# Weights of experts 2 and 3, gathered rows and one store at other places of the load queue

## The chip, the cores and the metric

The kernel runs on one core of a Trainium2 chip. The metric is the device time of one execution in microseconds (us). Three runs of the kernel before took 327.52, 327.14 and 326.27 us, median 327.14. The profile is of one further execution that took 327.53 us; its span, from the first to the last instruction, is 326.0 us.

## The reference

Attention with normalised q and k, then a mixture of experts in which a hash of the token's id picks the expert:

```python
q_n, k_n = rmsnorm(q, g_q), rmsnorm(k, g_k)          # q, k, v: 8 batches, 12 heads, 448 tokens, 64
attn = softmax(q_n @ k_n.T / 8)
x = (attn @ v) as rows                               # 8 * 448 = 3584 rows of 768
expert = token_ids * 2654435761 % 8
out[rows of e] = relu(x[rows of e] @ w1[e]) @ w2[e]  # 8 experts: w1 768 x 1024, w2 1024 x 768
```

Inputs are float32; the kernel computes in 16 bits and accumulates in float32.

## The kernel before, in words

**Two halves.** The first half is attention, in 48 steps of a pair of heads (six steps a batch). The order of its work is written out as lists of tokens (`steady`, and `tail` for the last batch, L944 to L965). A step s ends in `put_x` (L741); after the last step of a batch `store_x` (L753) writes its 448 rows of x to a scratch tensor in DRAM, in four pieces, all issued by SyncE (the queue SP), but for the last batch, where GpSimd (the queue POOL) issues two of the four. `put_x` then calls `hooks(s + 1)` (L846), which places loads: w1 and w2 of expert 0 at steps 24 and 27, of expert 1 at 30 and 33, w1 of expert 2 at 37. All weights are cast to 16 bits by their DMAs, and all of those are issued by POOL, in the order in which the program has them; a DMA that must wait holds back all that stand behind it on POOL.

**The second half** is a loop over the eight experts (L1304). An expert has at most 468 rows, in four blocks ("columns") of 128, 128, 128 and 84. The first three blocks hold rows of the first seven batches ("early rows"), the fourth also rows of the last batch ("late rows"). For each expert: `gemm1` (L1000) makes h = relu(x w1) in eight parts of six matmuls, each evicted from PSUM by ScalarE (`both=False`) or by ScalarE and VectorE in turn (`both=True`, for expert 7 alone); `gemm2` (L1027) makes the first three blocks of the output; `gemm2_across` (L1057) makes the 84 rows of the fourth, with 48 short matmuls of 84 columns, which VectorE then transposes (L1071). Each block is scattered to `out` by an indirect DMA from POOL (L1049). Expert 0 differs: its first three blocks run before the late rows are there, and `gemm1_late` (L988) adds the fourth.

**Rows.** `gather` (L237) fetches a block of an expert's rows by an indirect DMA from POOL. For the early rows of expert 0 it is called in `hooks` at steps 43 to 45, into `xg_e`, which is the memory of the first k buffer (`kr_0`); for those of expert 1 after the last token of attention (L968), into the ring `xg_ring`, the memory of the second k buffer (`kr_1`), whose eight places are shared by all experts. `fetch` (L1078) does it in the second half. TensorE turns the rows of experts 0 and 1 (`put_xT`, L246); for experts 2 to 6 VectorE does it in blocks (`turn_blocks`, L1104), and ScalarE sorts the result (`separate`, L1114), for the next expert, while the present one runs.

**Weights of the second half.** w1 and w2 of expert 2 lie in the memory of the first q and k buffers (`w_views`, L199), so w2 of 2 shares `kr_0` with `xg_e` and is loaded after the early rows of expert 0 have been turned (L1302). Experts 3 to 7 are loaded in five pieces each: `w_pieces(e)` queues them, and `w_next(n)` issues the next n, at fixed places between the scatters (L1317 to L1340). The POOL queue before, from the end of attention: store of the last batch, three gathers of expert 1, late rows of 0 and 1, w2 of 2 in three pieces, the scatters of expert 0 with the fetch of expert 2's rows and weights of 3 between them.

**TensorE** takes its matmuls in program order. `before` and `between` (L1293) say which block of rows is turned ahead of, or in the middle of, which block of expert 0's `gemm2`.

Of the kernel before, what the change touches and what calls it, by code (L numbers as in the profile page):

```python
# [20 lines left out]
def kernel(  # L21
# [12 lines left out]
    nc = tc.nc  # L34

    B, H, S, D = q.shape
    N, DIN = out.shape
    E = moe_w1.shape[0]
# [12 lines left out]
    FIT = 468  # L51
    LAST = FIT - 3 * P
    KT = CAP // P
# [29 lines left out]
    qk_keep = [m_xe.tile([P, RAW], FP16, name=f"{a}r_0") for a in "qk"]  # L83
    k_keep = m_xe.tile([P, RAW], FP16, name="kr_1")
    xg_ring = k_keep[:].rearrange("p (r d) -> p r d", d=DIN)
    xg_e = qk_keep[1][:].rearrange("p (r d) -> p r d", d=DIN)
    xT_e = m_xe.tile([P, CAP // P, CO, P], FP16, name="xT_e")

    nc.scalar.preload_act_table_set("natural_log_exp_and_others")
# [107 lines left out]
    w_tiles = {}  # L197
# [14 lines left out]
    def load_w1(e, w1_sb, dyn=None):  # L212
        src = moe_w1[e] if dyn is None else moe_w1[bass.ds(dyn, 1)].rearrange("o d f -> (o d) f")
        for c in range(0, CO, 2):
            nc.gpsimd.dma_start(out=w1_sb[:, c:c + 2], in_=w1_rows(src, c, e in PAIRED))
        return w1_sb

    def load_w2(e, w2_sb, dyn=None):
        src = moe_w2[e] if dyn is None else moe_w2[bass.ds(dyn, 1)].rearrange("o f d -> (o f) d")
        rows = "(fo p) d -> p fo d" if e == 0 else "(p fo) d -> p fo d"  # L220
        cuts = (0, FO // 2, 3 * FO // 4, FO) if e == 2 else (0, FO)
        for f, g in zip(cuts, cuts[1:]):
            nc.gpsimd.dma_start(out=w2_sb[:, f:g], in_=src.rearrange(rows, fo=FO)[:, f:g])
        return w2_sb
# [7 lines left out]
    gidx = rt_keep.tile([P, NHI], I32)  # L232
# [4 lines left out]
    def gather(xg, idx, rows=N):  # L237
        nc.gpsimd.indirect_dma_start(  # L238
            out=xg[0:idx.shape[0], :], out_offset=None, in_=x_dram[0:rows, :],
            in_offset=bass.IndirectOffsetOnAxis(ap=idx, axis=0),  # L240
            bounds_check=rows - 1, oob_is_err=False)
        return xg

    N_EARLY = (B - 1) * S
# [9 lines left out]
    NS = B * HP  # L254
# [18 lines left out]
    with tc.manual_schedule(), \  # L273
# [479 lines left out]
        def store_x(b):  # L753
            x_sb = xs.pop(b)
            r0 = b * S

            def rows(tok0, cnt, col, width):
                return bass.AP(tensor=x_dram.tensor, offset=(r0 + tok0) * DIN + col,
                               ap=[[SL * DIN, 64], [1, cnt * width]])
            nc.sync.dma_start(out=rows(0, 3, 0, DIN),  # L760
                              in_=x_sb[0:64, 0:6, :].rearrange("p a c -> p (a c)"))
            eng = nc.gpsimd if b == B - 1 else nc.sync
            eng.dma_start(out=rows(4, 3, 0, DIN),
                              in_=x_sb[64:P, 0:6, :].rearrange("p a c -> p (a c)"))
            nc.sync.dma_start(out=rows(3, 1, 0, HW), in_=x_sb[0:64, 6, :])
            eng.dma_start(out=rows(3, 1, HW, HW), in_=x_sb[64:P, 6, :])
# [79 lines left out]
        def hooks(s):  # L846
            if s >= NS:
                return
            b, hp = s // HP, s % HP
            for f in SIDE.get(s, ()):  # L850
                f()
            if s == HP:
                load(4, "q")
                load(3, "v")
                load(4, "kv")
            if hp == 3 and 1 <= b and b + 4 < B:
                load(b + 4, "qkv")
            if NS - 5 <= s < NS - 6 + KT:
                c = s - NS + 5
                gather(xg_e[:, c], gidx[:, c:c + 1], N_EARLY)  # L860
            if s == 24:
                w_tiles[0] = [load_w1(0, new_w1(w_pool))]
            if s == 27:
                w_tiles[0].append(load_w2(0, new_w2(w_pool)))
            if s == 30:
                w_tiles[1] = [load_w1(1, new_w1(w_pool))]
            if s == 33:
                w_tiles[1].append(load_w2(1, new_w2(w_pool)))
            if s == 37:
                w_tiles[2] = w_views()  # L870
                load_w1(2, w_tiles[2][0])

        group_ops = {
            "sqq": lambda g, *p: prep_sq(flag, g, 0, *p),
# [90 lines left out]
        """  # L965
        for b in range(2, B):
            emit(steady if b < B - 1 else tail, b)
        for c in range(KT, 2 * KT - 1):  # L968
            gather(xg_ring[:, c], gidx[:, c:c + 1], N_EARLY)


    with tc.manual_schedule(), \
         tc.tile_pool(name="w_pool2", bufs=1) as w_pool2, \
# [10 lines left out]
        def w1_view(e, w1_sb):  # L984
            return w1_sb[:].rearrange("p c (o f) -> p c o f" if e == 0 else "p c (f o) -> p c o f",
                                      o=FO)
# [89 lines left out]
        xTs = {0: xT_e}  # L1076

        def fetch(e, kts):  # L1078
            for kt in kts:
                c = e * KT + kt  # L1080
                xgs[c] = gather(xg_ring[:, c % (2 * KT)],
                                gidx[0:P if kt < KT - 1 else LAST, c:c + 1],
                                N_EARLY if kt < KT - 1 else N)
# [26 lines left out]
        def separate(e):  # L1110
            xw = xws.pop(e)
            xT = xTs[e] = m_x.tile([P, CO, CAP], FP16, name="xT")
            for c in range(CO // 2):
                nc.scalar.copy(xT[:, 2 * c:2 * c + 2, 0:FIT],  # L1114
                               xw[:, c, 0:FIT].rearrange("p t w -> p w t"))
# [8 lines left out]
        def w_pieces(e):  # L1124

            if e % 4 == 2:
                w1_sb, w2_sb = w_views()
            else:
                pool = w_pool if e % 4 < 2 else w_pool2
                w1_sb, w2_sb = new_w1(pool), new_w2(pool)  # L1130
            w_tiles[e] = (w1_sb, w2_sb)
            src2 = moe_w2[e].rearrange("(p fo) d -> p fo d", fo=FO)
            res = []
            for c in range(0, CO, 2):
                res.append((w1_sb[:, c:c + 2], w1_rows(moe_w1[e], c, e in PAIRED)))
            for q4 in range(0, FO, 4):
                res.append((w2_sb[:, q4:q4 + 4], src2[:, q4:q4 + 4]))
            return res

        queue = []  # L1140

        def w_next(n):
            for _ in range(min(n, len(queue))):
                o, i = queue.pop(0)
                nc.gpsimd.dma_start(out=o, in_=i)
# [145 lines left out]
        t = lambda e, kt: (lambda: turn(e, kt))  # L1291
        t0 = lambda e, kt: (lambda: turn(e, kt, nc.scalar.copy))
        before, between = {}, {}  # L1293
        before[0, 0], before[0, 1] = [t0(1, 0)], [t0(0, KT - 1)]
        between[0, 1] = t0(1, 1)
        before[0, 2] = [lambda: gemm1_late(w1_view(0, w_tiles[0][0]), xTs.pop(0), hs[0], EARLY, FIT)]
        between[0, 2] = t0(1, 2)
        before[0, 3] = [t(1, 3)]
        hs = {}
        fetch(0, [KT - 1])  # L1300
        fetch(1, [KT - 1])
        load_w2(2, w_tiles[2][1])  # L1302
        queue += w_pieces(3)
        for e in range(E):  # L1304
            w1_sb, w2_sb = w_tiles[e]
            h_sb = hs[e] = m_h.tile([P, FO, CAP], FP16, name="h_sb")
            after = [plan.get((e, "g", fo), []) for fo in range(FO)]
            if e == 0:
                gemm1(w1_view(e, w1_sb), xTs[e], h_sb, 0, EARLY, False, after, 2)
            else:  # L1310
                if e == E - 2:
                    turn_by_dma(E - 1)
                if e < E - 2:
                    fetch(e + 2, range(KT))
                    turn_blocks(e + 1)
                gemm1(w1_view(e, w1_sb), xTs.pop(e), h_sb, 0, FIT, e == E - 1, after)
            if e:  # L1317
                w_next(2)
            if e == 2:
                n_ov = nc.values_load(novi[0:1, 0:1], min_val=0, max_val=NOV)  # L1320
            if e == E - 1:
                nc.gpsimd.drain()
            for kt in range(KT):
                c = e * KT + kt
                for f in before.get((e, kt), []):
                    f()
                if kt == KT - 1 and 0 < e < E - 1:
                    gemm2_across(w2_sb, h_sb, gidx[:, c:c + 1])
                else:
                    gemm2(w2_sb, h_sb, kt, gidx[:, c:c + 1], between=between.get((e, kt)),  # L1330
                          last=(c == E * KT - 1), by_v=e in (0, E - 2, E - 1))
                for f in plan.get((e, "k", kt), []):
                    f()
                if kt == 1 and e + 1 in PAIRED:
                    separate(e + 1)
                if e or kt > 1:
                    w_next(1)
            w_next(len(queue))
            if e + 4 < E:
                queue += w_pieces(e + 4)  # L1340

        with tc.For_i(0, n_ov, 1) as it:  # L1342
            ex = nc.values_load(ov_i[0:1, bass.ds(it, 1)], engines=[mybir.EngineType.Pool],
                                min_val=0, max_val=E - 1)
            w1_sb = load_w1(None, new_w1(w_pool2), ex)
# [42 lines left out]
```

## Time and profile before

| what | value |
|---|---|
| profiled execution | 327.53 us |
| span of its instructions | 326.0 us |
| TensorE busy (matmul) | 312.1 us, 96% of the span |
| VectorE, ScalarE, GpSimd busy | 233.7, 217.9, 146.6 us |
| attention ends, expert 0 begins | 159.5 us |
| experts 1 to 7 begin | 182.8, 201.9, 221.0, 240.5, 260.1, 280.3, 299.5 us |
| last matmul ends, last scatter is issued | 320.1, 320.8 us |
| moved by DMA | 65.55 MB, mean 201 GB/s |

Busy times overlap. A matmul's end is modelled, so a TensorE that is shown busy may still be held up a little; a gap shown is real. The granted TensorE clock was full (1.0 in all stretches before 300 us).

### The profile page before, as it was taken

How to read it: one execution, taken by the hardware profiler on the slowest of the kernel's cores; microseconds unless marked ns; L12 is line 12 of the kernel's file. 1: busy time of each engine (PE TensorE's matmuls, PEld its weight loads, DVE VectorE, ACT ScalarE, POOL GpSimd, SP SyncE). 2: the span in 40 equal slices, each digit the busy share in tenths (PEclk: the TensorE clock that was granted, in tenths of full speed). 3: DMA queues.
4: the chain of work that ended last, by engine and by line, in shares of the span. 5: the costliest groups of instructions: out<-in, count | busy, mean ns of one | idle time of the engine just before them, and what ended most of it. 6: DMA issues, size and time to landing. Idle time of an engine off the chain costs nothing. (4 is left out here: it accounts for less than half of the span.)

```text
span 326.0 us, 9467 instructions
## 1 busy us (share of the span) xinstructions
PE 312.1 (96%) x3957; PEld 219.4 (67%) x3957; DVE 233.7 (72%) x530; ACT 217.9 (67%) x331; POOL 146.6 (45%) x207
## 2 busy tenths in 40 slices
PE   7799999999999999999999999999999999899992
PEld 3577777777777777565767767767676675767661
DVE  4799999898999999986596285865865659502610
ACT  4799999999999999999644345454363553641211
POOL 8799944432441100003176683552845648423122
PEclk9999999999999999999999999999999999999999
DMA  7999999999999999813259799999999999994013
GB/s 134 203 203 202 201 242 199 240 200 240 203 239 213 242 231 210 197 30 97 73 147 170 245 187 216 256 268 277 256 250 271 262 261 262 261 290 165 23 50 124
DMA packets 43683, 65.55 MB, mean 201 GB/s; under 512 B 12727, under 2 KB 33423, under 8 KB 43512
## 3 DMA queue, kind: packets, MB, share of 16 engines
q0 software_dynamic: 37152, 58.32, 87.7%
q1 hardware_dynamic: 6328, 6.50, 7.3%
q8 instruction: 31, 0.51, 0.6%
q10 hardware_dynamic: 160, 0.11, 0.1%
q14 instruction: 12, 0.10, 0.1%
HBM read 89.14 MB, written 17.01 MB: 326 GB/s over the span
## 5 line engine op out<-in xcount | busy, mean ns | idle before, releaser
L668 ACT ACTIVATE expT<-sc_ps 128x896 bf16<-128x896 f32 x144 | 125.1, 961 | 2.1 <-PE sc_ps L645 1.8
L1020 ACT ACTIVATE h_sb<-h_ps 128x468 f16<-128x468 f32 (+1 forms) x60 | 33.0, 551 | 48.1 <-PE h_ps L1011 43.6
L1049 POOL DMA_INDIRECT out_dram<-o_sb,gidx x32 | 35.3, 1102 | 53.7 <-DMA w_sb<-in_moe_w_dram 13.6
L1033 PEld LDWEIGHTS <-h_sb 128*128 128x128 f16 (+1 forms) x416 | 40.9, 99 | 26.8
L1104 DVE STREAM_TRANSPOSE xw<-kr 32x384 f32<-32x384 f32 (+1 forms) x80 | 43.6, 545 | 16.8 <-DMA kr<-x_scratch,gidx 15.8
L238 POOL DMA_INDIRECT kr<-x_scratch,gidx x32 | 32.9, 1029 | 49.0 <-DVE qT L637 36.9
L1033 PE MATMUL o_ps<-w_sb,h_sb 128*128 128x512 f16 (+3 forms) x320 | 53.8, 326 | 0.0
L1011 PEld LDWEIGHTS <-w_sb 128*128 128x128 f16 x300 | 39.4, 135 | 15.4 <-issue 0.9
L1011 PE MATMUL h_ps<-xT,w_sb 128*128 128x468 f16 x240 | 48.5, 361 | 0.4 <-DVE h_sb L1022 0.4
L645 PE MATMUL sc_ps<-qT,kT 64*128 64x448 f16 x288 | 44.4, 356 | 1.0 <-DVE qT L637 0.4
L686 PEld LDWEIGHTS <-expT 128*128 128x128 bf16 x846 | 36.8, 97 | 9.6 <-DVE x_sb L746 4.6
L686 PE MATMUL av_ps<-v,expT 128*128 128x65 bf16 x828 | 41.5, 193 | 0.3 <-DVE x_sb L746 0.2
L1043 ACT COPY o_sb<-o_ps 128x768 f32<-128x768 f32 x21 | 16.7, 797 | 33.6 <-PE o_ps L1033 29.6
L314 POOL DMA_DIRECT2D vr<-in_v_dram x36 | 23.6, 667 | 19.3 <-DMA kr<-in_k_dram 10.0
L746 DVE TENSOR_TENSOR x_sb<-av_ps,srec 128x448 f16<-128x448 f32 x47 | 29.3, 623 | 1.3
L671 ACT ACTIVATE expT<-sc_ps 128x448 bf16<-128x448 f32 x48 | 28.7, 600 | 0.1
L1071 DVE STREAM_TRANSPOSE o_sb<-o_ps 32x192 f32<-32x192 f32 x72 | 27.2, 378 | 1.1
L395 PEld LDWEIGHTS <-ident 128*128 128x128 f16 x576 | 22.6, 98 | 7.5 <-issue 2.5
L691 PE MATMUL av_ps<-v,expT 128*128 128x130 bf16 x138 | 24.0, 220 | 0.0
L1011 PE MATMUL h_ps<-xT,qr 128*128 128x468 f16 x96 | 19.3, 362 | 0.0
L645 PEld LDWEIGHTS <-kT 64*128 64x128 f16 x288 | 12.4, 93 | 9.8 <-issue 2.5
L648 PE MATMUL sc_ps<-qT,kT 128*128 128x448 f16 x48 | 16.9, 352 | 0.6 <-ACT expT L668 0.6
(233 smaller groups left out, 453.3 us busy)
## 6 DMA issues: line engine op xcount, KB each, us to landing
w_sb<-in_moe_w_dram POOLq DMA_DIRECT2D x18, 512.0 KB
w_sb<-in_moe_w_dram POOLq DMA_DIRECT2D x8, 768.0 KB
kr<-in_k_dram POOLq DMA_DIRECT2D x7, 672.0 KB
qr<-in_q_dram POOLq DMA_DIRECT2D x7, 672.0 KB
x_scratch<-x_sb SPq DMA_DIRECT2D x15, 288.0 KB, 6.7
w_sb<-in_moe_w_dram POOLq DMA_DIRECT2D x2, 1536.0 KB
qr<-in_moe_w_dram POOLq DMA_DIRECT2D x6, 512.0 KB
vr<-in_v_dram POOLq DMA_DIRECT2D x14, 192.0 KB
```

The lines of the kernel that those rows point to most:

```text
L238: nc.gpsimd.indirect_dma_start(out=xg[0:idx.shape[0], :], out_offset=None, in_=x_dram[0:rows, :], in_offset=bass.IndirectOffsetOnAxis(ap=i ...
L645: nc.tensor.matmul(sc[:, hh, :S], lhsT=kT[64 * hh:64 * hh + 64, P * j:P * j + P], rhs=qT[64 * hh:64 * hh + 64, :], start=True, stop=True)
L668: nc.scalar.activation(expT[:, 2 * j:2 * j + 2, :], sc[:, :, :S], AF.Exp, bias=0.0, scale=1.0)
L671: nc.scalar.activation(expT[:, 6, :], sc[:, 0, :S], AF.Exp, bias=0.0, scale=1.0)
L686: nc.tensor.matmul(av[:, 2 * t + hh, :], lhsT=expT[:, tl(hh, j), P * t:P * t + P], rhs=v8[:, i, vs(hh, j), 0:D + 1], start=(hh == 0 and t ...
L746: nc.vector.tensor_tensor(out=xs[b][:, :, hp * D:hp * D + D], in0=av[:, :, :D], in1=srec[:, :, None].to_broadcast([P, SL, D]), op=ALU.mult)
L1011: nc.tensor.matmul(dst, lhsT=w1v[:, co, fo, :], rhs=src, start=(co == 0), stop=(co == CO - 1))
L1020: nc.scalar.activation(h_sb[:, fo, c0:c1], h_ps[:, :c1 - c0], AF.Relu)
L1033: nc.tensor.matmul(o_ps[d0 > 0][0:w, d0:d1], lhsT=h_sb[:, fo, col * P:col * P + w], rhs=w2_sb[:, fo, d0:d1], start=(fo == 0), stop=(fo == ...
L1049: scat = nc.gpsimd.indirect_dma_start(out=out[:, :], out_offset=bass.IndirectOffsetOnAxis(ap=idx[0:w], axis=0), in_=o_sb[0:w], in_offset=N ...
L1071: nc.vector.transpose(out=dst[t0:t0 + 32, m], in_=src[32 * m:32 * m + 32, :, t0:t0 + 32])
L1104: nc.vector.transpose(out=dst[32 * m:32 * m + 32, :, g].rearrange("p c k r -> p k c r"), in_=xg[32 * i:32 * i + 32, 0:n, m])
```

## The change

Six edits. w2 of expert 2 is loaded at step 37, behind its w1. For that, the early rows of expert 0 go into the ring instead of `kr_0`. The early rows of expert 1 are gathered at step 46 instead of behind the last step. In the second half two pieces of expert 3's weights are issued ahead of the late rows and the other three behind them, ahead of expert 0's first scatter, and the first two pieces of expert 4 follow at its third and fourth block; the fourth block of expert 0 is turned one place later and the second of expert 1 one place earlier. The store of batch 6 is split between SP and POOL as that of batch 7 was. And expert 7's `gemm1` no longer evicts in turn: ScalarE does all eight parts.

```diff
-    xg_e = qk_keep[1][:].rearrange("p (r d) -> p r d", d=DIN)
+    xg_e = xg_ring
...
-            eng = nc.gpsimd if b == B - 1 else nc.sync
+            eng = nc.gpsimd if b >= B - 2 else nc.sync
...
+            if s == NS - 2:
+                for c in range(KT, 2 * KT - 1):
+                    gather(xg_ring[:, c], gidx[:, c:c + 1], N_EARLY)
...
                 load_w1(2, w_tiles[2][0])
+                load_w2(2, w_tiles[2][1])
...
-        for c in range(KT, 2 * KT - 1):
-            gather(xg_ring[:, c], gidx[:, c:c + 1], N_EARLY)
...
-        before[0, 0], before[0, 1] = [t0(1, 0)], [t0(0, KT - 1)]
-        between[0, 1] = t0(1, 1)
+        before[0, 0], before[0, 1] = [t0(1, 0)], [t0(1, 1)]
+        between[0, 1] = t0(0, KT - 1)
...
+        queue += w_pieces(3)
+        w_next(2)
         fetch(0, [KT - 1])
         fetch(1, [KT - 1])
-        load_w2(2, w_tiles[2][1])
-        queue += w_pieces(3)
...
             if e == 0:
+                w_next(len(queue))
                 gemm1(w1_view(e, w1_sb), xTs[e], h_sb, 0, EARLY, False, after, 2)
...
-                gemm1(w1_view(e, w1_sb), xTs.pop(e), h_sb, 0, FIT, e == E - 1, after)
+                gemm1(w1_view(e, w1_sb), xTs.pop(e), h_sb, 0, FIT, False, after)
...
+                if e == 0 and kt == 2:
+                    queue += w_pieces(4)
                 if e or kt > 1:
                     w_next(1)
-            w_next(len(queue))
-            if e + 4 < E:
-                queue += w_pieces(e + 4)
+            if e:
+                w_next(len(queue))
+                if e + 4 < E:
+                    queue += w_pieces(e + 4)
```

## Rows read from the trace of the kernel before

**Rows 1.** Windows: us, each engine's busy (x instructions), TensorE clock, DMA share, GB/s
```profile
201.85:220.97 19.12, 19.12 (x150) 13.36 (x146) 13.37 (x29) 9.39 (x14) 9.86 (x11) 1.00 1.05 261
220.97:240.50 19.53, 19.29 (x150) 13.41 (x146) 13.37 (x29) 8.44 (x13) 11.01 (x13) 1.00 1.04 262
240.50:260.14 19.64, 19.29 (x148) 13.43 (x146) 13.37 (x29) 9.24 (x15) 11.02 (x13) 1.00 1.05 261
260.14:280.33 20.19, 19.29 (x148) 13.48 (x146) 13.37 (x29) 10.16 (x16) 11.64 (x13) 1.00 1.07 261
299.45:309.51 10.06, 9.66 (x53) 6.88 (x50) 6.50 (x16) 2.24 (x4) 1.45 (x2) 1.00 0.14 52
```
**Rows 2.** Waits over the span: us in total, times, longest us
```profile
POOL out_dram L1049 <- DMA w_sb<-in_moe_w_dram: 13.6, 5, 4.3
...
PE o_ps L1061 <- issue: 1.5, 3, 0.9
...
PE h_ps L1011 <- DVE h_sb L1022: 0.4, 1, 0.4
```
**Rows 3.** Timeline of TensorE: start, us, line, count [idle before, releaser]
```profile
211.36 7.96 PE L1033 MATMUL o_ps<-kr,h_sb 128*128 128x512 f16 x48
219.16 1.98 PE L1061 MATMUL o_ps<-h_sb,kr 128*128 128x84 f16 x48
...
240.34 0.32 PE L1061 MATMUL o_ps<-h_sb,w_sb 128*128 128x84 f16 x4 [0.24 <-issue]
...
279.95 0.54 PE L1061 MATMUL o_ps<-h_sb,w_sb 128*128 128x84 f16 x10 [0.90 <-issue]
```
**Rows 4.** Timeline of GpSimd, a scatter of expert 1 and last gathers of two fetches
```profile
211.28 0.99 POOL L1049 DMA_INDIRECT out_dram<-o_sb,gidx  x1 [0.36 <-issue]
...
218.21 1.02 POOL L238 DMA_INDIRECT kr<-x_scratch,gidx  x1 [0.30 <-issue]
...
238.61 1.02 POOL L238 DMA_INDIRECT kr<-x_scratch,gidx  x1 [0.30 <-issue]
```
**Rows 5.** Timeline of VectorE, rows of experts 4 and 6 turned in blocks
```profile
229.13 8.91 DVE L1104 STREAM_TRANSPOSE xw<-kr 32x384 f32<-32x384 f32 x16 [3.01 <-DMA kr<-x_scratch,gidx]
...
268.55 8.92 DVE L1104 STREAM_TRANSPOSE xw<-kr 32x384 f32<-32x384 f32 x16 [3.25 <-DMA kr<-x_scratch,gidx]
```
**Rows 6.** Timeline of ScalarE, rows of experts 3 and 6 sorted
```profile
217.45 2.72 ACT L1114 COPY xT<-xw 128x936 f16<-128x936 f16 x3
...
277.55 2.72 ACT L1114 COPY xT<-xw 128x936 f16<-128x936 f16 x3 [1.66 <-DVE xw L1104]
```
**Rows 7.** Timeline of VectorE in expert 7's `gemm1`: transposes, then its evictions
```profile
300.54 4.69 DVE L1071 STREAM_TRANSPOSE o_sb<-o_ps 32x192 f32<-32x192 f32 x12
...
305.26 1.20 DVE L1022 TENSOR_SCALAR h_sb<-h_ps 128x468 f16<-128x468 f32 x2
```
**Rows 8.** Page, part 6: a piece of w1; part 3: the instructions' own DMA queue
```profile
w_sb<-in_moe_w_dram POOLq DMA_DIRECT2D x18, 512.0 KB
...
q8 instruction: 31, 0.51, 0.6%
```
**Rows 9.** Timeline of GpSimd from the loads in attention to the late rows
```profile
113.24 1.05 POOL L215 DMA_DIRECT2D qr<-in_moe_w_dram  x2 [11.69 <-DVE n_q L443]
151.21 1.11 POOL L238 DMA_INDIRECT kr<-x_scratch,gidx  x1 [36.91 <-DVE qT L637]
...
167.51 1.02 POOL L238 DMA_INDIRECT kr<-x_scratch,gidx  x1 [0.72 <-issue]
```
**Rows 10.** All instructions on the scratch tensor: time to landing of SyncE's stores
```profile
DMA to landing us min/median/max: 2.1/7.1/9.9
```
**Rows 11.** Windows as in rows 1, where the DMA engines have room
```profile
138.00:144.00 6.00, 5.99 (x119) 4.16 (x118) 5.75 (x15) 6.00 (x9) 0.00 (x0) 1.00 0.03 7
...
163.00:170.00 7.00, 7.00 (x48) 4.20 (x47) 6.38 (x22) 2.94 (x6) 5.25 (x5) 1.00 0.61 161
```
**Rows 12.** Timeline of TensorE, expert 0's rows turned: first block, fourth block
```profile
156.00 0.49 PE L250 MATMUL sc_ps<-ident,kr 128*128 128x128 f16 x6
...
171.29 0.39 PE L250 MATMUL xT_ps<-ident,kr 84*128 84x84 f16 x6 [0.18 <-ACT xT L252]
```

## The prediction

> **What bounds the kernel now.** I read the page first: TensorE is busy in 312 of 326 us, so anything the change moves counts only where TensorE stands still. The chain of waits names only the last scatter, so the gaps are read elsewhere: the waits say who made TensorE stop, the windows by expert what each stop costs, the timelines of the other engines what they did then. The waits show three stops after attention that matter: 1.5 us in three pieces inside the short matmuls of `gemm2_across`, with no releaser in the profile ("issue"), and 0.4 us for an eviction by VectorE [rows 2]. The windows price them. Expert 2, which has no stop, takes 19.12 us; experts 3, 4 and 5 take 19.53, 19.64 and 20.19, so the three stops cost 0.41 + 0.52 + 1.07 = 2.00 us [rows 1]. Expert 7's `gemm1` takes 10.06 us [rows 1]; the same 48 matmuls of expert 2 take 211.36 - 201.85 = 9.51 [rows 1, 3], so that stop costs 0.55 us. Nothing else of size is there to win: TensorE waits for no weights and no late row.
>
> The DMA engines are the other full resource: from 202 to 280 us their share is 1.04 to 1.07 at 261 GB/s [rows 1]. GpSimd's queue feels this: its scatters wait for a weight's landing five times, 13.6 us in all [rows 2], and the gathers behind them are issued late. VectorE then waits 3 us for the rows of the next expert [rows 5]. So far that lies beside TensorE's work, but barely: ScalarE sorts the rows of expert 3 from 217.45 to 220.17, 0.80 us before that expert begins at 220.97, and those of expert 6 from 277.55 to 280.27, 0.06 us before 280.33 [rows 1, 6].
>
> **The change part by part.**
>
> *ScalarE evicts all of expert 7's h.* VectorE's two first evictions come at 305.26, because it transposes from 300.54 to 305.23 [rows 7]; TensorE runs out of PSUM banks meanwhile. ScalarE needs 2.24/4 = 0.56 us for a part [rows 1] and one comes every 9.51/8 = 1.19 us, so it keeps up, and it has nothing else queued there. This removes the whole stop: -0.55 us, with bounds -0.40 (the idle time shown, rows 2) and -0.56 (adding the slower restart). VectorE's saved work lies beside TensorE's.
>
> *w2 of expert 2 at step 37.* It has the size of w1, three pieces of 512 KB [rows 8], 1.57 MB. On GpSimd it stands behind w1 of 2, whose last pieces were issued at 113.24, when the q of batch 5 had been used [rows 9]; the k was used before that in the token list, so no new wait stands there, and GpSimd has nothing to do until the gathers at 151. The DMA engines are idle from 138 to 144 (share 0.03) [rows 11]; 1.57 MB at 0.261 MB/us is 6.0 us, which fills just this hole. Cost 0. If the cover is gone, the gathers of expert 0 come late: they were issued from 151.21 [rows 9], and TensorE turned the first at 156.00 without a stop [rows 12]. With the whole 6 us of loading ahead of them they would come 151.2 + 1.1 + 2.1 (shortest landing, rows 10) + 6 = 160.4, so the bounds are 0 and +4.4; I take 0, since the hole has the size of the load.
>
> *Half of batch 6's store on GpSimd; rows of expert 0 in the ring; rows of 1 at step 46.* The gathers of expert 0 waited on GpSimd for that store alone, until 151.21 [rows 9]. Split in two, it can land a microsecond or so sooner, and the gathers of expert 1 then follow directly, some 9 us earlier than before. TensorE waits for none of these, so I take 0. GpSimd's two store pieces stand behind w2 of 2 and ahead of these gathers only; the expert 1 gathers stand ahead of batch 7's store, which comes later than they do. If the split store landed no sooner, or up to the 9.9 us of rows 10 after its issue, nothing would change before 155, when the first gather would still be in time within 2 us: bounds 0 and +2.
>
> *Weights of 3 around the late rows.* Before, GpSimd did the late gathers from 167.51, when the last store had landed [rows 9], and the DMA engines had room (share 0.61 from 163 to 170, rows 11). Now two pieces (1.05 MB, 4.0 us at the rate of rows 1) go into that hole from about 163. The late gathers stand behind them but still wait for the store, so they are issued at 167 to 168 as before and their data queue behind at most a rest of these pieces. TensorE asked for expert 0's fourth block at 171.29 [rows 12]; it now comes after the second block of expert 1 and half a block of `gemm2`, at about 171.29 + 0.5 + 1.6 = 173.4. I take a landing at 170 to 171 and so 0. One thing gets tighter: `gemm1_late` begins at about 174.5, and ScalarE's copy of that block, done well before until now, then ends just there: bounds 0 and +0.3; I take +0.05. The 0.18 us stop at 171.29 stays: it waits for the same copy.
>
> *What the queue gains.* All of expert 3 (3.15 MB) is issued before the first scatter, and w2 of 2 before the end of attention, where w2 of 2 alone (1.57 MB) went in that time before. The DMA engines begin expert 1 with 3.15 MB less to do: 3.15/0.261 = 12 us of lead. An expert moves 3.15 MB of weights, 468 x 1536 B of rows and 468 x 3072 B of results, 5.30 MB or 20.3 us, against 19.1 us of TensorE: the lead shrinks by 1.2 us an expert and lasts past expert 5. So GpSimd no longer waits for landings. A `fetch` stands behind the fourth scatter of the expert before, which needs the last transposes of VectorE (about 5.2 us into the expert). Scatter and four gathers then take 1 + 4 x 1.3 us, so the last gather is issued some 11.5 us into an expert instead of 17.6 (238.61 - 220.97) [rows 1, 4]. VectorE's 3 us waits [rows 5] go, and the rows are sorted some 2 us sooner.
>
> *Does this remove the three stops?* No row names their releaser. What they share: in experts 3, 4 and 5 the last gather of the fetch is issued into the short matmuls (238.61 to 239.63, then a stop that ends at 240.34; the other two look the same) and ScalarE sorts at the same time with nothing to spare. In expert 2, whose last gather is issued by 219.23, as the short matmuls start at 219.16, and whose rows are sorted from 217.45, there is none [rows 3, 4, 6]; expert 1 is earlier still. The change puts experts 3 to 5 ahead of expert 2's position. Bounds: 0 if the cause is something else, -2.00 if all go; I take -2.00, as the row nearest to the new state is expert 2's.
>
> The Trainium skill speaks against this step. "Runtime: NRT & Kernel Launch", section "Instruction fetch mechanics", says that an engine's instructions come in blocks of 16 KiB by its own DMA queue, and that crossing a block costs little and mostly out of sight. If the three stops were such crossings, they would stay, as the change leaves TensorE's instructions nearly as they are, and the sum would be 327.0. The page's queue 8 has 31 transfers and 0.51 MB, so blocks of that size are in this trace [rows 8]; whether a stop falls on one, no row shows.
>
> Sum, against the profiled execution's 327.53: -0.55 - 2.00 + 0.05 = -2.50, so 325.0. The median of the runs is 327.14, 0.4 below; some of the stops may be smaller there, so I leave 325.0 and do not take the 0.4 off as well.
>
> **The rivals.**
>
> *A. The stops in `gemm2_across` stay* (0.33). They have no releaser in the profile, and a wait for the sorted rows would show on the first matmul that reads them, not a few matmuls ahead. Then only expert 7 gains: 327.53 - 0.50 = 327.0. Against it stands the order of experts 1 to 6: a stop exactly where gather and sorting are late.
>
> *B. Late rows are late (slower)* (0.08). The place is expert 0's fourth block. If SyncE's half of the last store, which takes up to 9.9 us to land in a full DMA phase [rows 10], is held up by the new pieces, the late gathers are issued at 171 and land behind the three other pieces' start; or their data take turns with all of expert 3's. That load takes 3.15/0.261 = 12.1 us from 163, to 175, and a landing 2.1 us later (the shortest shown, rows 10) is 177.2: TensorE, in order, stands from 173.4, 3.8 us. With the stops gone it is 328.8, with the stops left 330.8. It decides against the kernel from a landing at 173.4 + 2.5 = 175.9 on. Against it: the DMA engines had 39% free in this stretch, and only two of five pieces stand ahead of the gathers.
>
> *C. The change does not do what it says* (0.05): a wait of the new early loads, for memory that attention still uses, holds GpSimd, and the queue is as late as before. Then 327.0 again, by expert 7 alone.
>
> **How the numbers follow.** Forecast 0.54 at 325.0, own range 324.2 to 325.8; A 0.33 and C 0.05 at 327.0 (326.4 to 327.5); B 0.08 at 328.8 to 330.8. The range that leaves out B and the far ends: 324.2 to 327.5. About 0.5% (1.6 us) can be told from no change. Faster by that means below 325.5: most of the forecast and a little of A in which one or two stops go, 0.53; slower means B, without its mild part, 0.07; the rest, 0.40, is within it.
>
> **What would show it.** Right: expert 7's `gemm1` in 9.5 us; experts 3 to 5 in 19.1 us each; no DVE wait before the block transposes of experts 4 to 6; last gathers of a fetch about 12 us into an expert; w2 of 2 loaded by 144; the DMA share from 163 to 170 near 1. Wrong: stops without releaser in `gemm2_across` as long as before although the gathers are early (A); a TensorE wait for a DMA at the turning of the fourth block (B); GpSimd idle ahead of its first weights of expert 3 (C).

## The result and the profile after

The kernel after takes 330.68 us, median of six runs (330.01 to 330.94); the kernel before, on the same chip, 327.36. The ratio is 1.0086, 95% interval 1.0057 to 1.0116. That is slower by 2.8 us (by 3.3 us if the two medians are compared), where 2.5 us less were forecast. The profiled execution of after took 330.94 us, span 329.3 us. Lines from L1011 on have a number one higher in after (L1012 for L1011, L1105 for L1104, L1146 for L1145); in experiments 1, 4, 6 and 9 they have the old one, in experiment 11 one that is three higher.

First the windows of after by stage, with the columns of [rows 1]: the stretch in which attention ended before (159.52) and ends now (164.88), then experts 0, 1, 3 and 5 and expert 7's `gemm1`.

```profile
159.52:164.88 5.36, 4.53 (x55) 3.53 (x54) 2.68 (x6) 3.55 (x5) 0.20 (x1) 0.51 1.01 198
164.88:188.52 23.64, 23.45 (x241) 16.66 (x238) 15.90 (x39) 9.40 (x18) 11.79 (x11) 0.97 0.70 141
188.52:207.61 19.09, 19.09 (x146) 13.35 (x145) 10.70 (x20) 9.39 (x14) 13.24 (x16) 1.00 0.97 237
...
226.73:245.86 19.13, 19.13 (x150) 13.42 (x146) 13.37 (x29) 9.39 (x14) 10.85 (x13) 1.00 1.04 265
...
264.98:284.10 19.12, 19.12 (x150) 13.39 (x146) 13.37 (x29) 9.39 (x14) 9.99 (x11) 1.00 1.04 278
...
303.22:312.73 9.51, 9.51 (x54) 6.86 (x51) 4.66 (x13) 3.92 (x7) 1.45 (x2) 1.00 0.15 55
```

Everything forecast from expert 1 on is there: experts 3 and 5 take 19.13 and 19.12 us where they took 19.53 and 20.19, and expert 7's `gemm1` takes 9.51 instead of 10.06 [rows 1]. Experts 1 to 7 gained 2.5 us. But expert 0 begins 5.36 us later than before and takes 0.40 us longer (23.64; before, 182.76 - 159.52 = 23.24). The waits of after from 150 to 165 us (us in total, times, longest; "remote" means that the profile finds no instruction that sent the awaited signal, "issue" that it shows nothing that was waited for):

```profile
DVE srec L738 <- remote: 5.7, 1, 5.7
ACT expT L668 <- remote: 4.5, 1, 4.5
...
PE sc_ps L250 <- issue: 2.2, 2, 1.1
```

and TensorE's timeline there, which answers to [rows 12]:

```profile
153.87 0.54 PE L686 MATMUL av_ps<-v,expT 128*128 128x65 bf16 x12 [0.77 <-PE sc_ps L648]
...
158.06 0.38 PE L250 MATMUL sc_ps<-ident,kr 128*128 128x128 f16 x4 [1.13 <-issue]
159.48 0.27 PE L250 MATMUL sc_ps<-ident,kr 128*128 128x128 f16 x2 [1.04 <-issue]
160.59 0.56 PE L645 MATMUL sc_ps<-qT,kT 64*128 64x448 f16 x2 [0.83 <-ACT expT L668]
```

TensorE stops several times around the turning of expert 0's first block, mostly with no releaser, and VectorE and ScalarE wait 5.7 and 4.5 us, by their tiles for signals of matmuls that were done by 155.5. Its clock falls next, from 1.00 to the lower of its two levels (0.50); windows of after:

```profile
157.00:159.00 2.00, 0.38 (x4) 0.39 (x5) 0.00 (x0) 0.00 (x0) 1.70 (x3) 1.00 0.50 171
159.00:161.00 2.00, 0.69 (x4) 0.30 (x3) 1.29 (x3) 1.38 (x2) 0.72 (x2) 0.66 0.82 147
161.00:163.00 2.00, 2.00 (x28) 1.65 (x27) 1.16 (x3) 1.59 (x3) 0.00 (x0) 0.50 1.09 219
...
165.00:167.00 2.00, 2.00 (x13) 1.50 (x13) 0.82 (x2) 0.10 (x1) 0.85 (x2) 0.64 0.28 54
```

GpSimd's timeline, which answers to [rows 9], shows what is new in that stretch: six gathers and two weight pieces of expert 3 (L1146) in one unbroken run, all of it ahead of the last batch's store (L763).

```profile
150.88 1.12 POOL L238 DMA_INDIRECT kr<-x_scratch,gidx  x1 [4.31 <-DVE oc L587]
...
157.53 0.99 POOL L238 DMA_INDIRECT kr<-x_scratch,gidx  x1 [0.30 <-issue]
158.52 1.20 POOL L1146 DMA_DIRECT2D w_sb<-in_moe_w_dram  x2
166.15 0.55 POOL L763 DMA_DIRECT2D x_scratch<-x_sb  x1 [6.43 <-DVE x_sb L746]
...
172.84 1.06 POOL L238 DMA_INDIRECT kr<-x_scratch,gidx  x1 [5.60 <-DMA x_scratch<-x_sb]
...
175.24 1.74 POOL L1146 DMA_DIRECT2D w_sb<-in_moe_w_dram  x3
```

One more row matters later: VectorE turns the rows of expert 2 from 195.03, after a wait of 5.36 us for them. The gathers of these rows were issued from 187.53, some 5 us later than in the traces below, as expert 0 began late. TensorE, late itself, did not notice.

```profile
195.03 8.91 DVE L1105 STREAM_TRANSPOSE xw<-kr 32x384 f32<-32x384 f32 x16 [5.36 <-DMA kr<-x_scratch,gidx]
```

### The profile page after: what moved, and what is told of

It is laid out like the page before. It is cut to its first block, busy times and chain, and to the rows that moved or that the text cites. A ratio compares the mean times of both kernels' runs of the same rounds, so it can differ in the third digit from the quotient of the medians.

```text
span 329.3 us, 9467 instructions
## 1 busy us (share of the span) xinstructions
PE 314.1 (95%) x3957; PEld 220.7 (67%) x3957; DVE 230.5 (70%) x526; ACT 219.9 (67%) x335; POOL 147.4 (45%) x209
## 5 line engine op out<-in xcount | busy, mean ns | idle before, releaser
L1021 ACT ACTIVATE h_sb<-h_ps 128x468 f16<-128x468 f32 (+1 forms) x64 | 35.3, 551 | 50.0 <-PE h_ps L1012 46.8
L1012 PEld LDWEIGHTS <-w_sb 128*128 128x128 f16 x300 | 39.8, 136 | 15.3 <-issue 0.3
L1012 PE MATMUL h_ps<-xT,w_sb 128*128 128x468 f16 x240 | 48.3, 361 | 0.0
L1105 DVE STREAM_TRANSPOSE xw<-kr 32x384 f32<-32x384 f32 (+1 forms) x80 | 43.6, 545 | 6.5 <-DMA kr<-x_scratch,gidx 5.4
L238 POOL DMA_INDIRECT kr<-x_scratch,gidx x32 | 32.6, 1019 | 19.1 <-issue 8.8
L1068 DVE MEMSET o_ps<- 128x72 f32 x6 | 0.7, 118 | 28.3 <-ACT o_sb L1044 15.3
L1012 PE MATMUL h_ps<-xT,qr 128*128 128x468 f16 x96 | 19.3, 362 | 0.0
```

The source lines that it names most:

```text
L238: nc.gpsimd.indirect_dma_start(out=xg[0:idx.shape[0], :], out_offset=None, in_=x_dram[0:rows, :], in_offset=bass.IndirectOffsetOnAxis(ap=i ...
L1012: nc.tensor.matmul(dst, lhsT=w1v[:, co, fo, :], rhs=src, start=(co == 0), stop=(co == CO - 1))
L1021: nc.scalar.activation(h_sb[:, fo, c0:c1], h_ps[:, :c1 - c0], AF.Relu)
L1105: nc.vector.transpose(out=dst[32 * m:32 * m + 32, :, g].rearrange("p c k r -> p k c r"), in_=xg[32 * i:32 * i + 32, 0:n, m])
```

## The experiments

Ratios are to the kernel before on the same chip. Expert 0 begins between 158.06 and 161.20 us in the traces below, none of which has the stops just shown, so beside the ratios stands the **second half** of the profiled execution: from the start of expert 0 to the end of the span. It is 326.0 - 159.5 = 166.5 us for before and 329.3 - 164.9 = 164.4 for after.

### 1. Is it the run of gathers? Rows of 1 back

```diff
-            if s == NS - 2:
-                for c in range(KT, 2 * KT - 1):
-                    gather(xg_ring[:, c], gidx[:, c:c + 1], N_EARLY)
...
             emit(steady if b < B - 1 else tail, b)
+        for c in range(KT, 2 * KT - 1):
+            gather(xg_ring[:, c], gidx[:, c:c + 1], N_EARLY)
```

> The kernel after with one step undone: the three early row gathers of expert 1 stand behind the attention loop again, as in the kernel before; all else of the change stays. Theory G (a long unbroken run of row gathers on GpSimd keeps TensorE's matmuls from starting and its semaphores from arriving until it ends): only three gathers of expert 0 stand in the end of attention, so attention ends near 159.5 us (before: 159.52; after: 164.88), the granted clock doesn't fall, and the rest of the change is kept: 327.4 - 2.0 - 0.55 = 324.8 us, up to 326 if the two weight issues that now follow the gathers directly hold TensorE as gathers do. Theory W (the two weight pieces of expert 3, 1.05 MB moved at 158.5 us, are what disturbs TensorE): these pieces now move some 4 us earlier, the loss stays: about 330 us, with the stop near 156 to 158. Theory R (the rows of experts 0 and 1 in one ring tensor make TensorE wait for the later gathers): 324.8 us, as under G.

324.73 us, ratio 0.9949 (0.9918 to 0.998); expert 0 begins at 159.71, second half 163.8 us, clock 0.996. The loss is gone and most of the gain stays, as theories G and R said: by the medians 1.9 us less than the kernel before, where they said 2.6. W falls, since the weight pieces stood at 155.22 with no harm.

### 2. Weight pieces of 3 behind the late rows

```diff
-        w_next(2)
         fetch(0, [KT - 1])
         fetch(1, [KT - 1])
+        w_next(2)
```

> The kernel after with the first two weight pieces of expert 3 put behind the late rows of experts 0 and 1, so that the six gathers stand alone in the end of attention. Theory G (gathers): TensorE is still held until about 158.5 to 159.5 us, 329.5 to 331 us. Theory W (weight pieces): the loss of 5.4 us at the end of attention goes, 325 us. Theory R (shared ring tensor): as the kernel after, 330.7 us.

328.57 us, ratio 1.0064 (1.0034 to 1.0094). A miss for all three: expert 0 begins at 159.03, so six gathers alone, in the shared ring, hold up nothing, and G and R fall too. The time is lost elsewhere. All five pieces of expert 3 are issued together from 167.99, behind the late rows; expert 2 waits 1.60 us for its sorted rows, and experts 1 and 2 take 20.9 and 21.5 us.

### 3 and 4. Two steps alone, put into the kernel before

The gathers of expert 1 at step 46 (the lines taken out in experiment 1, put into before):

> The kernel before with one step of the change alone: the three early row gathers of expert 1 are issued at step 46, directly behind those of expert 0. The rows of expert 0 keep their own tensor, and no weights of expert 3 are near. Theory G (gathers): TensorE is held at the turning of expert 0's first block until some 0.8 us after the sixth gather, about 159.5 us instead of 155.7, and its clock falls as in the kernel after: 327.4 + 3.8 + 1.6 = 332.5 us, from 331 to 333. Theory W and theory R: no change, 327.4 us.

326.55 us, ratio 0.9983 (0.995 to 1.0016); expert 0 begins at 158.98. G falls here as well.

Expert 7's evictions:

```diff
-                gemm1(w1_view(e, w1_sb), xTs.pop(e), h_sb, 0, FIT, e == E - 1, after)
+                gemm1(w1_view(e, w1_sb), xTs.pop(e), h_sb, 0, FIT, False, after)
```

> The kernel before with one edit of the change alone: ScalarE evicts all of expert 7's h. All theories: expert 7's gemm1 takes 9.51 us instead of 10.06, so 326.8 us; nothing else moves, and the stops of experts 3 to 5 stay at 19.53, 19.64 and 20.19 us.

326.28 us, ratio 0.9986 (0.996 to 1.0012): -0.35 us by the medians, not told from nothing. In its trace expert 7's `gemm1` takes 9.51 us, as forecast. The stops at the end of experts 3 to 5 are not there, but what they cost has moved to the start of experts 4 to 6. Windows of experts 4, 5 and 6 of this run, then TensorE's timeline at the start of expert 5:

```profile
238.28:257.74 19.46, 19.39 (x149) 13.50 (x146) 13.38 (x29) 8.81 (x15) 10.68 (x13) 1.00 1.04 263
257.74:277.87 20.13, 19.49 (x146) 13.44 (x145) 13.37 (x29) 9.51 (x15) 11.48 (x14) 1.00 1.07 261
277.87:298.12 20.25, 19.58 (x148) 13.41 (x145) 5.61 (x14) 8.49 (x13) 7.20 (x8) 1.00 0.92 246
```

```profile
258.62 0.55 PE L1011 MATMUL h_ps<-xT,w_sb 128*128 128x468 f16 x2 [0.32 <-ACT xT L1114]
259.49 8.85 PE L1011 MATMUL h_ps<-xT,w_sb 128*128 128x468 f16 x44 [0.32 <-ACT xT L1114]
```

No stop in `gemm2_across` is left; the next expert's first matmuls wait for ScalarE's sorted rows instead. The three experts take 2.5 us more than three times 19.12, where the stops of the kernel before cost 2.00. So the late rows are a floor under these experts. That the stops without releaser of the first trace stood in front of the same floor and hid it is likely, but not shown.

### 5 and 6. After again; both steps back

After, unchanged, and the edits of experiments 1 and 2 together.

> The kernel after, unchanged, profiled and timed once more beside kernels that undo parts of it. The six gathers alone and the weight pieces behind three gathers left attention without a stop. Theory K (what holds TensorE is the whole unbroken run, six gathers and then two weight issues): the stop comes back, expert 0 begins near 164.9 us, the clock falls to 0.986 in the mean, and the time is 330 to 331 us. Theory C (the stop belongs to an execution or a chip, not to the order of GpSimd's work): expert 0 begins near 159.2 us, the clock stays at 0.995 or more, and the time is 325 to 327 us.

328.67 us, ratio 1.0061 (1.0036 to 1.0087). Theory C was right about attention (expert 0 at 159.79, no stop without releaser) and wrong about the time. The profiled execution took 330.34 us at a mean clock of 0.989; eight of the twelve took 327.55 to 329.11 us at 0.995 or more. As the unchanged kernel can run without the stops of attention, their absence in experiments 1 to 3 does not decide between G, W and R. TensorE's timeline, at expert 0's fourth block and at the start of expert 2:

```profile
174.15 0.40 PE L250 MATMUL xT_ps<-ident,kr 84*128 84x84 f16 x6 [0.71 <-DMA kr<-x_scratch,gidx]
204.98 0.56 PE L1012 MATMUL h_ps<-xT,qr 128*128 128x468 f16 x2 [2.16 <-ACT xT L1115]
```

and the windows behind that second stop, where the clock falls:

```profile
206.00:208.00 2.00, 2.00 (x6) 0.80 (x5) 1.93 (x6) 1.61 (x3) 0.34 (x1) 0.50 0.96 138
208.00:210.00 2.00, 2.00 (x9) 1.09 (x8) 1.91 (x6) 0.66 (x2) 0.67 (x1) 0.72 1.00 265
```

Expert 1 takes 21.41 us, expert 2 21.21: 2.3 us for the stop, 2.1 us for a further one of 0.32 and the low clock behind it. VectorE turned the rows of 2 from 195.01, after a wait of 10.29 us. That the first trace has nearly the same time (195.03) is chance: the gathers were issued from 182.58 here and from 187.53 there.

> The kernel after with both steps undone: the early rows of expert 1 behind the attention loop, and the first two weight pieces of expert 3 behind the late rows. What is left of the change: w2 of 2 in attention, batch 6's store split, rows of 0 in the ring, the order of the turns, the evictions of expert 7. Theory K: no stop in attention; if only the pieces of expert 3 ahead of the late rows give the queue its lead, expert 2 begins late as in the run with the pieces behind (some 1.7 us of waiting for sorted rows, and a lower clock after it), about 328.5 us; if the lead of w2 of 2 is enough, 324.7 us. Theory C: the same two numbers.

327.76 us, ratio 1.0041 (1.002 to 1.0061). The first of the two numbers (1.0041 times the 327.4 us of the first measurement is 328.7): rows of 2 turned from 193.21, a stop of 2.07 us at expert 2, second half 168.3 us. The lead of w2 of 2 alone is not enough. In this run, with no weights ahead of it, SyncE's part of the last store lands in 3.1 us, and so it does in experiment 2, which differs from after in the place of the two pieces alone; in experiment 5, behind the two pieces, it lands in 8.5 us. DMA issues of experiment 5, then of experiment 6 (KB each, us to landing):

```profile
x_scratch<-x_sb SPq DMA_DIRECT2D x1, 288.0 KB, 8.5
```

```profile
x_scratch<-x_sb SPq DMA_DIRECT2D x1, 288.0 KB, 3.1
```

### 7, 8 and 9. The pieces of 3 behind the rows of 2

The last three pieces behind the gathers of expert 2:

```diff
             if e == 0:
-                w_next(len(queue))
...
                 if e == 0 and kt == 2:
+                    w_next(len(queue))
                     queue += w_pieces(4)
```

> The kernel after with the last three weight pieces of expert 3 (2.1 MB) put behind the row gathers of expert 2; the first two stay ahead of the late rows. Theory Q (these pieces stand in the DMA queue ahead of expert 2's rows, so the rows are sorted late, TensorE stops about 2 us at expert 2 and its clock falls for as long again): the rows of 2 are transposed from about 189 us instead of 195, the stop and the low clock go, experts 1 and 2 take 19.1 us each, and the time falls by about 4 us in the executions that had the stop, to 324.5 to 326; what remains is a fraction of a microsecond for the late rows, which still wait for the store. Theory P (the gathers of 2 are late because GpSimd comes to them late): they are issued some 1.7 us sooner, the stop shrinks to about 0.5 us, 327. Theory S (only the stops at the end of attention count): no change, 328 to 331.

327.12 us, ratio 1.0012 (0.9978 to 1.0046). The mechanism is as Q says: rows of 2 turned from 190.90 with a wait of 4.85 us as before, no stop at expert 2, 19.1 us each from expert 1 on; a wait of 0.63 us for the late rows remains. The second half is 164.5 us, 3.5 to 4.5 below experiments 10 and 5. The gathers of 2 are no sooner than in experiments 5 and 10 (183.91 against 182.58 and 182.84), so it is not P's mechanism, though the time is the one that P gave: it fell by less than Q said. The profiled execution began expert 0 late, at 161.20. It was late from its start, far ahead of the place that the edit moves: in the first 20 us TensorE is busy for 14.4 us, in experiment 10 for 16.4. Why is not known.

All five pieces behind the gathers of 2 (the edit above, and `w_next(2)` ahead of the late rows taken out):

> The kernel after with all five weight pieces of expert 3 (3.15 MB) behind the row gathers of expert 2. Theory Q: as the run above, and as nothing stands ahead of batch 7's store, it lands in about 4 us instead of 8.8, the late rows are gathered near 165.6 us instead of 171, and expert 0 takes 22.9 us; 324.5 us, or up to 1 us more if the pieces, now together, delay the rows of expert 3. Theory P: 326 to 327. Theory S: no change, 328 to 331.

329.67 us, ratio 1.0071 (1.0047 to 1.0095). Half a hit: the late rows are gathered at 165.40, expert 0 takes 22.9 us, the rows of 2 are turned from 187.61. But the pieces now stand ahead of the rows of expert 3, far worse than the 1 us allowed for. VectorE and TensorE there, and the window of expert 3:

```profile
212.89 8.92 DVE L1105 STREAM_TRANSPOSE xw<-kr 32x384 f32<-32x384 f32 x16 [6.92 <-DMA kr<-x_scratch,gidx]
```

```profile
222.92 12.72 PE L1012 MATMUL h_ps<-xT,w_sb 128*128 128x468 f16 x48 [2.82 <-DMA out_dram<-o_sb,gidx]
```

```profile
222.92:245.08 22.16, 22.16 (x144) 13.67 (x144) 12.34 (x26) 11.80 (x17) 12.14 (x15) 0.86 1.02 248
```

The profile puts the stop down to a scatter, but ScalarE's first sorted rows come just then: it begins to sort them at 221.89, after a wait of 5.38 us for VectorE. The same loss, one expert on: a stop of 2.82 us, then 22.16 us instead of 19.12 with TensorE busy throughout and its clock at 0.86 in the mean.

Both repairs (experiments 1 and 7):

> The kernel after with the rows of expert 1 back behind attention and the last three weight pieces of expert 3 behind the rows of expert 2: the two repairs together. Theory Q: both repairs give the rows of 2 a lead, each is enough alone, so the time is that of the first experiment's kernel, 0.994 to 0.995 of before, 324.5 us; no stop above 0.3 us after attention. Theory S: the same. A result clearly below, near 323 us, would mean that the first experiment's kernel still paid for late rows in some executions.

324.64 us, ratio 0.9928 (0.989 to 0.9966), second half 163.8 us: the fastest kernel of the study, though its interval overlaps that of experiment 1. GpSimd's timeline:

```profile
154.75 1.19 POOL L1145 DMA_DIRECT2D w_sb<-in_moe_w_dram  x2
160.56 0.55 POOL L763 DMA_DIRECT2D x_scratch<-x_sb  x1 [4.62 <-DVE x_sb L746]
...
167.78 1.90 POOL L238 DMA_INDIRECT kr<-x_scratch,gidx  x1 [2.13 <-DMA x_scratch<-x_sb]
```

### 10 and 11. After a third time; nine gathers

> The kernel after, unchanged, in a third place, to see which of its two losses is the rule: the stops without releaser at the end of attention (first trace: expert 0 begins at 164.9 us, clock 0.986) or the late rows of expert 2 (second trace: expert 0 begins at 159.8, TensorE waits 2.2 us at expert 2, clock 0.989). Theory Q (the late rows of expert 2 are the loss, and the stops at the end of attention an accident of some executions): expert 0 begins at 158.8 to 160 us if the start of the program is as usual, a stop of about 2 us at expert 2, ratio 1.006. Theory G (gathers hold TensorE): expert 0 begins at 163 us or later and expert 2 without a stop, ratio 1.008 or more.

328.81 us, ratio 1.0063 (1.0034 to 1.0093): theory Q. Expert 0 begins at 159.10. GpSimd's timeline, and the windows of experts 0, 1 and 2:

```profile
158.34 1.20 POOL L1146 DMA_DIRECT2D w_sb<-in_moe_w_dram  x2
160.36 0.55 POOL L763 DMA_DIRECT2D x_scratch<-x_sb  x1 [0.82 <-DVE x_sb L746]
...
171.04 1.48 POOL L238 DMA_INDIRECT kr<-x_scratch,gidx  x1 [9.59 <-DMA x_scratch<-x_sb]
...
174.19 1.75 POOL L1146 DMA_DIRECT2D w_sb<-in_moe_w_dram  x3
```

```profile
159.10:183.83 24.73, 22.88 (x242) 16.17 (x238) 15.68 (x39) 9.67 (x18) 10.84 (x12) 1.00 0.75 154
183.83:204.44 20.61, 19.26 (x147) 13.47 (x145) 10.62 (x20) 7.10 (x12) 13.21 (x16) 1.00 1.00 246
204.44:224.49 20.05, 19.41 (x145) 13.36 (x145) 13.44 (x30) 11.79 (x17) 10.46 (x12) 1.00 1.00 239
```

Here the chain is whole: pieces at 158.34, store behind them, late rows gathered at 171.04 after 9.59 us of waiting, the other three pieces at 174.19, and only then the rows of 2, gathered from 182.84 and turned from 194.47. TensorE waits at expert 0's fourth block and at expert 2:

```profile
174.42 0.40 PE L250 MATMUL xT_ps<-ident,kr 84*128 84x84 f16 x6 [1.67 <-DMA kr<-x_scratch,gidx]
204.44 0.56 PE L1012 MATMUL h_ps<-xT,qr 128*128 128x468 f16 x2 [1.35 <-ACT xT L1115]
```

VectorE's turning of the rows of 2 in the kernel before, in experiment 10, and in experiment 7, where the three pieces stand behind these rows:

```profile
188.67 8.91 DVE L1104 STREAM_TRANSPOSE xw<-kr 32x384 f32<-32x384 f32 x16 [4.76 <-DMA kr<-x_scratch,gidx]
```

```profile
194.47 8.91 DVE L1105 STREAM_TRANSPOSE xw<-kr 32x384 f32<-32x384 f32 x16 [9.48 <-DMA kr<-x_scratch,gidx]
```

```profile
190.90 8.91 DVE L1105 STREAM_TRANSPOSE xw<-kr 32x384 f32<-32x384 f32 x16 [4.85 <-DMA kr<-x_scratch,gidx]
```

Against the 22.90, 19.09 and 19.12 us of experiment 9 the three experts lose 1.83, 1.52 and 0.93 us.

Three gathers of expert 1 issued twice, in the kernel of experiment 3:

```diff
                 for c in range(KT, 2 * KT - 1):
                     gather(xg_ring[:, c], gidx[:, c:c + 1], N_EARLY)
+                for c in range(KT, 2 * KT - 1):
+                    gather(xg_ring[:, c - KT], gidx[:, c:c + 1], N_EARLY)
```

> The kernel before with the three early gathers of expert 1 directly behind those of expert 0 and, behind these, the same three once more into free places of the ring, which nobody reads: nine gathers in one unbroken run through the end of attention, half as many again as in the kernel after. The three added gathers leave the output as it is. Theory G (issuing gathers holds TensorE's short matmuls): a stop at the end of attention that lasts to the end of the run, expert 0 begins at 163 us or later, 332 us. Theory Q: TensorE doesn't stop in attention, expert 0 begins near 159 us; the last store of GpSimd comes some 3 us later than in the third experiment, so the late rows come later too, at worst with a wait of 1 to 2 us at expert 0's fourth block: 326.5 to 328.5 us.

328.16 us, ratio 1.0037 (1.0006 to 1.0067); expert 0 begins at 159.21. Nine gathers end at 162.75 and TensorE does not stop in attention; the cost is the late rows, as Q said. TensorE's timeline:

```profile
172.78 0.40 PE L250 MATMUL xT_ps<-ident,kr 84*128 84x84 f16 x6 [1.97 <-DMA kr<-x_scratch,gidx]
```

## Why the prediction was wrong

**Steps that held.** ScalarE's evictions for expert 7: -0.55 us in the trace, as forecast; alone, it was too small to be told in the times (experiment 4). The three stops of experts 3 to 5: gone in all versions with the early w2 of 2 and early pieces of 3 (19.1 us each in the first trace and in experiments 1, 7, 9, 10). Loading w2 of 2 in attention cost nothing that the traces show (issued from 115.04 to 120.75 us in the first trace), though its pieces have 768, 384 and 384 KB, and not 512 each. Splitting batch 6's store gained nothing: the gathers of expert 0 are issued from 150.88 where they were from 151.21, and both rows name VectorE, and not the store, as what ended the wait. Without the losses below, the second half is 163.8 us (experiments 1 and 9), against 166.5 - 2.5 = 164.0 from the sum.

**Rival A.** The stops did not stay. They were no crossings of instruction blocks either: from 238 to 241 us of the kernel before, round the stop that ends at 240.34, only the software queue moves anything, and the same holds from 258 to 260.5 and from 278 to 280, round the two others:

```profile
## 3 DMA queue, kind: packets, MB, share of 16 engines
q0 software_dynamic: 159, 0.80, 104.1%
```

So the rule weighed in the prediction (the Trainium skill, "Runtime: NRT & Kernel Launch", "Instruction fetch mechanics") does not explain them. What bounds those experts where no such stop is seen is the lateness of their sorted rows (experiments 4 and 11).

**The step that failed first: "Weights of 3 around the late rows", taken at +0.05 us.** It put the two pieces at about 163 us, behind the last store, and the late gathers at 167 to 168. The source has the pieces behind that store, but in every trace of after they are issued ahead of it: at 158.3 to 158.8, 1.05 MB, with the store at 160.4 to 161.1 behind them (experiments 5 and 10). Why the order on GpSimd is not that of the source is not known. The store lands some 9 us after its issue instead of 3 to 4 (experiment 2), and the late rows are gathered at 171.0 (experiments 5 and 10), which is what rival B said, with a chance of 0.08. The stop at expert 0's fourth block that B priced at 3.8 us was 0.71 and 1.67 us. Step 46 has its part: the three early gathers of expert 1, costed at 0, hold GpSimd longer and push the pieces from 154.75 (experiment 9) to 158.34, right onto the store. Without these gathers (experiment 1), or without the pieces ahead of the store (experiment 2), TensorE does not wait for the late rows.

The Trainium skill, "DMA: Bandwidth & Descriptors", section "Issuing engines are not separate DMA queues", says that transfers of all issuing engines share the same 16 DMA engines and interleave; SyncE's store, 3.1 us alone and 8.5 behind GpSimd's pieces, agrees.

**The step that failed with the larger price: "What the queue gains".** It counted 3.15 MB less to load after expert 1 begins, 12 us of lead, and asked only whether GpSimd would still wait. It did not ask who stands behind the moved bytes. The last three pieces of expert 3, 2.1 MB, are issued at 174 to 175 us, behind the late rows and 8 us ahead of the gathers of expert 2, where 1.57 MB stood, issued from 170.1, before. The rows of 2 are turned from 195.01 and 194.47 us (experiments 5 and 10), instead of 188.67. Expert 2 then begins at 204.98 and 204.44, after a stop: 1.5 us of loss without a fall of the clock (experiment 10, and 0.9 in expert 2's first matmuls), 4.4 us with one (experiment 5). In experiment 1 the same three pieces stand ahead of the rows of 2 as well, but are issued at 171.16, three to four us sooner, as the late rows are, and expert 2 does not stop. Put behind the rows of 2, the pieces cost nothing at expert 2 (experiment 7); all five there, they strike the rows of expert 3 (experiment 8); all five together behind the late rows, issued from 168.0 to 168.2, they strike expert 2 again (experiments 2 and 6). From expert 2 on the DMA engines are full [rows 1], and a lead has to be laid where no rows are due.

**What stays open.** The stops without releaser at the end of attention in the first trace, 5.4 us with the low clock behind them. In all six runs of after that were timed with it the mean clock was 0.985 to 0.990, so they or something like them may have been in each; but experiment 5's profiled execution comes to 330.34 us at 0.989 by the stop at expert 2, without them, so the times and the clock do not tell the two apart. Two further profiles of the same kernel do not have them. The order of the program alone does not make them, as these two run the same program. Gathers alone did not bring them (experiments 2, 3 and 11), and the weight pieces come too late for them: these are issued at 158.5, after the signals had been late since 155. The trace of before has its stops without releaser in `gemm2_across` [rows 2, 3], and none of the eleven traces taken later, on four chips, has one from 140 us on. What makes them, the chip or something else, is not shown. They are not the rule: the two executions of after without them stop at expert 2, and that kernel is slower by 0.6% all the same (experiments 5 and 10).

**The range.** It ended at 327.5, on the ground that B alone could pass it, at 0.08. B's place had a second price downstream that no rival held, and a stop of some 2 us was charged once, where experiment 5 paid for it twice.

## What to carry to other kernels

Where the DMA engines are full, a load moved forward is a load put ahead of something: list each transfer that will stand behind it, with the time at which its reader needs it, before counting a lead. Read the order in the issuing engine's queue from a trace, and not from the place of the line in the source. A stop without a releaser is not a sum to be won until another execution shows it too; look for the wait that it hides.

## What was not expected of the hardware

Some stops of TensorE were paid twice. Behind stops of 2.16 and 0.32 us (experiment 5) the granted clock was 0.50 from 206 to 208 us and 0.72 from 208 to 210, and expert 2 took 2.1 us more; behind 2.82 us (experiment 8) it was 0.50 from 222.92 to 229, and the next expert took 3.0 us more; behind 1.60, 0.32 and 0.27 us (experiment 2) it was 0.51 from 204 to 206. Behind 1.35, 0.32 and 0.32 us (experiment 10) the clock stayed at 1.00.

In the first trace of after, ScalarE and VectorE began at 159.5 to 159.6 on the results of matmuls that, by the profile, were done by 155.5; in the trace of experiment 10 such waits are not there.
